# The turn from attention to the experts in a fused attention, soft mixture and gated layer: another order of its last round, and output weights that no longer stay on chip

## The chip, the cores and the metric

The kernel runs on one core of one Trainium2 chip. The metric is the device time of one execution in microseconds (us), as the median of several runs; lower is better. The core has TensorE for matrix products (PE below, with PEld for its weight loads), VectorE (DVE), ScalarE (ACT), GpSimd (POOL) and SyncE (SP), which issues all the transfers of this kernel. PE writes to PSUM alone; POOL does not reach PSUM.

## The reference

Three layers, one after the other. Attention with pooled queries (4 batches, 8 heads, 1152 keys, 576 pooled queries, 64 wide), a soft mixture of 8 experts of 4 slots each on 2304 tokens of 512, and a gated layer of width 1536 with a root-mean-square norm ahead of it:

```python
q_pool = q.reshape(B, H, S // 2, 2, D).mean(axis=3)
scores = scale * np.matmul(q_pool, k.transpose(0, 1, 3, 2))
scores = scores - np.max(scores, axis=-1, keepdims=True)
attn = np.exp(scores); attn = attn / (np.sum(attn, axis=-1, keepdims=True) + 1e-09)
x = heads_joined(np.matmul(attn, v))                  # 2304 x 512

logits = x @ phi                                      # 2304 x 32 slots
d = softmax over the tokens; slot_input = d.T @ x
slot_out[e] = np.maximum(slot_input[e] @ w1[e], 0.0) @ w2[e]
x = (softmax over the slots of logits) @ slot_out

xn = x / np.sqrt(np.mean(x * x, -1, keepdims=True) + 1e-06) * rms_g
g = xn @ w_gate
out = (g * (1.0 / (1.0 + np.exp(-g))) * (xn @ w_val)) @ w_out
```

All is float32. Products that need the full width are split by the kernel into a high and a low part, each rounded for PE's fast float32 form (fp32r), and are put together from two or three passes.

## The kernel before

**Attention** runs in 16 rounds, one for each pair of heads. In a round the scores (`sc`, L401) are taken tile by tile, ACT takes their exponentials (`e`, L403), PE multiplies these with the values (`av`, L424), and POOL, in the last round DVE too, adds them up for the sums (`acc`, L418). The work of the round before (its division, its logits) and the loads are hung into a round at places from a table of due times (`AT`). When the last round is over there is a stretch that nothing overlaps, here called the **turn**: it sums up the last round (`sums`), takes the last logits (`xl`, `by`, `z`, `lgt`), makes the last part of the softmax over the tokens (`dtx`, `dn`), multiplies it with the attention's output `xt` (`xo` is that output turned, L919 and L492 divide it) to the slot inputs (`pp`, `psb`, `pto`), and adds the earlier parts (`pt`, `mxw`).

**The experts** follow, one after another: a product with `w1` (`hin`, L984), a turn of the hidden row (`hto`, into a zeroed tile `hz`) and a product with `w2` (`so`, L1009). Between them PE turns the tokens' softmax for the next layer (`c4o`).

**The gated layer** comes last. The squares of its inputs (`x`, L1037, by DVE or ACT), their root (`rs`, POOL), the scaled weights of the tokens (`pt`, `c`, DVE and ACT), the gate and value weights for the slots (`part`, `sgo`, L1150 and L1157), the gate (`gv`, `th`, `hu`, its parts `hA`, `hW` and `hC`, L1202) and the products with the output weights (`yo`, L1219). An order written out by hand, `SEQ`, sets the first of its six groups of tokens: `p` is a pair of gate weights (`part`), `x` a square, `r` the root and scaled weights, `c` the turn of these, `o` the other half of a pair (`sgo`), `g` a gate, `y` the output product, `t` a call that issues loads, `s` a split of one output weight block into its parts `woh` and `wol`.

**The loads** all go through SP in one order. A block is 128 x 512 float32 (256 KB). The 128 expert blocks come in a stream, `w1` and `w2` of the experts in turn. Gate, value and output weights arrive as 64-bit numbers during attention and are narrowed there. What does not stay on chip is written to device memory (`away`) and read back behind the expert blocks. Before the change the output weights 0 to 3 stay on chip (`HELD_O`), so 32 of 36 narrowed blocks go out and come back. Room on chip is counted in buffers of four kinds: A, B, C and W. `KEEP` says how many B buffers are left free at a call of `load`. In the turn `load(40)` stands twice: behind `take_x`, with the tighter room of the last round, and behind `slot_copy`, which frees the two W buffers that held `xt`. In the expert stage four output blocks are split ahead (`EARLY`): their high parts on ACT (L1082), the low parts on POOL (L1083).

Of the kernel before, what the change touches and what calls it, by code (L numbers as in the profile page):

```python
# [113 lines left out]
SQ_DVE = (0, 2)  # L114
SP_ACT = (0, 1, 5, 4, 3, 2)
SEQ = "p0 t x0 x1 x2 x3 p1 t r o0 o1 p2 t c g0 o2 g1 p3 t g2 g3 y0 t y1 g4 s p4 t y2 g5 s o3 y3 s t s g6 s p5 y4 g7 o4 t o5 y5 g8 y6 g9 s g10 s y7 s y8 g11 s y9 y10 y11".split()
# [10 lines left out]
EARLY = 4  # L127
LEAD = 1
KEEP = [10, 6, 12, 12]
KEEP_A = [2, 0]  # L130
HELD = 0
HELD_O = 4
AHEAD_O = -1
# [10 lines left out]
def attention_softmoe_gated_kernel(ctx: ExitStack, tc: tile.TileContext, kT, qT, vv, ip, cst, w1, w2, wg, wv, wo, rg, out):  # L144
# [96 lines left out]
    def accum(name):  # L241
        return ps.tile([128, 512], F32, tag="av", bufs=2, name=name)

# [474 lines left out]
    def side(p):  # L718
# [69 lines left out]
        if p == NP - 1:  # L788
            at("load_15", lambda i: (keep_b.__setitem__(0, KEEP[0]), load(1, KEEP_A[1])))
        return sorted(todo, key=lambda x: x[:2])  # L790

    with tc.manual_schedule():
# [92 lines left out]
        l = NP - 1  # L885
        sums(l)
        take_x(l)
        load(40)
        recips(l)
        x_logits(l)  # L890
        o = xl.pop(l)
        xs = B([128, HQ], F32, "xs")
        ac.copy(xs, o)
# [3 lines left out]
        o = bank([128, HQ], "by")  # L897
        for t in range(3):
            for h in range(2):
                for i in range(2):  # L900
                    g = 64 * h + 32 * i
                    pe.matmul(o[g:g + 32, TB * t:TB * t + TB], lhsT=r[:, h, t, i:i + 1].to_broadcast([TB, 32]), rhs=ident[0:TB, 0:TB], start=True, stop=True)
        z = B([128, HQ], F32, "z")
        dv.tensor_tensor(out=z, in0=o, in1=xs, op=ALU.mult)
        rel("B", 2)
# [8 lines left out]
        x_turn_all(l)  # L914
        d_add(z, False)
        for i in range(3):
            for s in range(2):
                c = slice(64 * s, 64 * s + 64)
                ac.activation(xts[0][:, i, l % 4, c], xo[l, i][0][:, i, c], AF.Copy, scale=r[:, 0, i, s:s + 1])  # L919
# [3 lines left out]
        x_divide(l, range(3, 6))  # L923
        rel("B")
# [7 lines left out]
        d_copy(3)  # L932

# [28 lines left out]
        load(40)  # L962
        o = bank([128, 4, 32], "pto")
# [113 lines left out]
        def split_w():  # L1077
# [4 lines left out]
            ac.copy(woh[i], x)  # L1082
# [3 lines left out]
        def pull(n=0):  # L1086
            for _ in range(n):
                split_w()
            load(64)
# [5 lines left out]
        for e in range(NE):  # L1095
# [4 lines left out]
            if e + 1 < NE:  # L1100
                hs = expert_in(e + 1, lambda: z.append(expert_mid(e, last)))
                pull(EARLY // 2 if e > NE - 4 else 0)
# [140 lines left out]
        for step in SEQ:  # L1243
# [13 lines left out]
            elif step[0] == "t":  # L1257
                load(64)
            elif step[0] == "s":
# [56 lines left out]
```

## Time and profile before

| what | value |
|---|---|
| median of the runs before (3 runs) | 712.32 us (712.07 to 714.51) |
| profiled execution, its own time | 713.79 us |
| span of that execution, first to last instruction | 711.8 us |
| PE busy | 691.3 us (97%) |
| DVE, ACT, POOL busy | 456.6, 392.7, 434.5 us |
| mean granted clock of PE | 0.992 of 2.4 GHz |
| attention ends, the turn begins | about 451 us |
| first expert product starts | 466.15 us |
| last expert product ends | about 509.4 us |
| all gated work of one group after another, PE without idle time | from 529 us on |

A row of the timeline gives the start, the length, the engine, the line, the operation, and in brackets how long the engine stood idle before it and what ended that. Records of PE overlap, so the distance between two starts says more than a length. PEclk in a table of stretches is the granted clock as a share of 2.4 GHz: 1.00 is 2.4 GHz and 0.50 is 1.2 GHz. The DMA share is the mean busy share of the 16 DMA engines and can come out just above 1.

### The profile page before, as it was taken

The numbers are of one execution on the slowest core, as the hardware profiler recorded it, in microseconds if no ns is written. First come the engines' busy times: TensorE is split into PE (matmuls) and PEld (weight loads), VectorE is DVE, ScalarE is ACT, GpSimd is POOL, SyncE is SP. The second block draws the span as 40 slices with busy tenths as digits, with TensorE's granted clock in tenths as the row PEclk, the third lists the DMA queues.
The fourth block names the chain that finished last, engine by engine and source line by source line (L and its number), as shares of the span: only waits on it lengthen the run. The fifth ranks groups of instructions, "written<-read, shape, count | busy, mean of one in ns | idle before, by whom it ended". The sixth has DMA issues, their size and how long they took to land.

```text
span 711.8 us, 15218 instructions
## 1 busy us (share of the span) xinstructions
PE 691.3 (97%) x5948; PEld 481.8 (68%) x5948; DVE 456.6 (64%) x661; ACT 392.7 (55%) x831; POOL 434.5 (61%) x351
## 2 busy tenths in 40 slices
PE   4999999999999999999999999899999999999998
PEld 2566666666676666666666676454367888888887
DVE  5667888887877897787887766321255755534420
ACT  2465666766566766657756534423266855454420
POOL 5578888877787877787887675001237854534420
PEclk9999999999999999999999999889999999999999
DMA  5041642843844844835624416399970100000000
GB/s 181 21 180 59 218 143 93 292 143 107 307 143 137 270 136 138 283 118 186 204 92 158 154 48 224 120 352 389 387 264 1 44 30 17 29 30 31 23 34 34
DMA packets 53000, 103.57 MB, mean 145 GB/s; under 512 B 5832, under 2 KB 19648, under 8 KB 52928
## 3 DMA queue, kind: packets, MB, share of 16 engines
q1 hardware_dynamic: 52928, 102.59, 41.8%
q8 instruction: 47, 0.77, 0.5%
q14 instruction: 25, 0.20, 0.1%
HBM read 89.39 MB, written 13.11 MB: 144 GB/s over the span
## 4 chain that ended last, share of the span: by engine, by line
PE 92%; issue 2%; DVE 2%; DMA 1%; ACT 1%; POOL 1%; SPq 0%; POOLq 0%; ACTq 0%; DVEq 0%
PE sc L401 23%; PE av L424 21%; PE yo L1219 21%; PE mxp L344 5%; PE gv L1171 4%; PE hin L984 2%; PE xo L483 2%; PE so L1009 2%; PE sums L449 1%; PE xl L500 1%; PE mxp L354 1%; PE pp L562 1%; PE mxp L350 1%; DMA qraw<-in_qT_dram 1%; PE sumt L459 1%
## 5 line engine op out<-in xcount | busy, mean ns | idle before, releaser
L418 POOL TENSOR_TENSOR acc<-acc,e 128x576 f32<-128x576 f32 x153 | 215.3, 1427 | 32.9 <-ACT e L403 28.7
L403 ACT ACTIVATE e<-sc 128x576 f32<-128x576 f32 x288 | 163.8, 657 | 64.6 <-PE sc L401 63.8
L345 DVE TENSOR_REDUCE mx<-mxp 128x2 f32<-128x1024 f32 x120 | 143.8, 1223 | 61.5 <-PE mxp L344 61.0
L424 PE MATMUL av<-e,vt 128*64 128x288 f32 x1152 | 167.8, 417 | 0.0
L418 POOL TENSOR_TENSOR acc<-e 128x576 f32<-128x576 f32 x63 | 94.0, 1502 | 73.6 <-ACT e L403 73.5
L424 PEld LDWEIGHTS av<-e,vt 128*64 128x64 f32 x1152 | 72.6, 136 | 63.7 <-issue 28.9
L1219 PE MATMUL yo<-woh,hA 128*128 128x512 f32 (+1 forms) x312 | 98.9, 384 | 0.0
L401 PE MATMUL sc<-qh,kh 64*128 64x288 f32 x576 | 93.5, 321 | 0.4 <-ACT mrow L370 0.4
L401 PE MATMUL sc<-mr,pick 64*128 64x288 f32 x576 | 85.7, 294 | 0.0
L401 PE MATMUL sc<-qh,kl 64*128 64x288 f32 x576 | 85.7, 293 | 0.0
L401 PE MATMUL sc<-ql,kh 64*128 64x288 f32 x576 | 85.6, 293 | 0.0
L1176 DVE SCALAR_TENSOR_TENSOR th<-th,gv 128x384 f32<-128x384 f32 x72 | 39.9, 554 | 62.4 <-ACT th L1173 61.9
L1202 POOL TENSOR_TENSOR hA<-hu,hA 128x384 fp32r<-128x384 f32 x48 | 48.8, 1018 | 42.9 <-ACT hA L1201 39.2
L401 PEld LDWEIGHTS sc<-qh,kh 64*128 64x128 f32 x576 | 54.5, 185 | 19.3 <-issue 6.6
L1219 PEld LDWEIGHTS yo<-woh,hA 128*128 128x128 f32 x312 | 57.6, 188 | 10.2 <-issue 0.7
L1173 ACT ACTIVATE th<-gv 128x384 f32<-128x384 f32 x72 | 35.2, 489 | 42.4 <-PE gv L1171 39.7
L1219 PE MATMUL yo<-wol,hA 128*128 128x512 f32 (+1 forms) x151 | 57.8, 383 | 0.0
L401 PEld LDWEIGHTS sc<-qh,kl 64*128 64x128 f32 x576 | 55.0, 187 | 0.0
L401 PEld LDWEIGHTS sc<-mr,pick 64*128 64x128 f32 x576 | 54.8, 186 | 0.0
L401 PEld LDWEIGHTS sc<-ql,kh 64*128 64x128 f32 x576 | 54.7, 186 | 0.0
L344 PE MATMUL mxp<-kh,qh 64*128 64x512 f32 x240 | 47.8, 436 | 0.2 <-ACT kh L283 0.2
L1178 DVE SCALAR_TENSOR_TENSOR hu<-th,gv 128x384 f32<-128x384 f32 x72 | 39.9, 554 | 8.1 <-PE gv L1171 0.5
(198 smaller groups left out, 1044.5 us busy)
## 6 DMA issues: line engine op xcount, KB each, us to landing
w<-in_w_dram SPq DMA_DIRECT2D x88, 256.0 KB
w<-in_w_dram SPq DMA_DIRECT2D x20, 512.0 KB
vt<-in_vv_dram SPq DMA_DIRECT2D x16, 576.0 KB
qraw<-in_qT_dram SPq DMA_DIRECT2D x15, 576.0 KB
kraw<-in_kT_dram SPq DMA_DIRECT2D x15, 576.0 KB
away<-w SPq DMA_DIRECT2D x32, 256.0 KB
w<-away SPq DMA_DIRECT2D x32, 256.0 KB
raw<-in_wg_dram SPq DMA_DIRECT2D x12, 512.0 KB
```

The costliest lines, as they stand in the source:

```text
L344: pe.matmul(o[:, s, :], lhsT=q[r, 128 * t:128 * t + 128], rhs=k[r, 512 * c:512 * c + 512], start=True, stop=True)
L345: dv.reduce_max(out=heads[:, :, t, c], in_=o, axis=AX.X)
L401: pe.matmul(o[:, s, 0:HQ], lhsT=w[r, wk], rhs=q[r, c], start=(i == 0), stop=(i == 3))
L403: ac.activation(ets[p, kt, h], o[:, :, 0:HQ], AF.Exp, scale=0.0625)
L418: eng.tensor_tensor(out=acc[p, h, j], in0=first[p, h, j] if n == 1 else acc[p, h, j], in1=e, op=ALU.add)
L424: pe.matmul(avt[p, h][64 * s:64 * s + 64, 0:HQ], lhsT=vt[p][:, kt, 64 * s:64 * s + 64], rhs=ets[p, kt, h][:, s], start=(kt == 0), stop=(kt ...
L1171: pe.matmul(o[i], lhsT=sg[n][:, 256 * i + 128 * c:256 * i + 128 * c + 128], rhs=cT[g], start=True, stop=True)
L1173: ac.activation(t, o[0], AF.Tanh, scale=0.5)
L1176: dv.scalar_tensor_tensor(out=t, in0=t, scalar=1.0, in1=o[0], op0=ALU.add, op1=ALU.mult)
L1178: dv.scalar_tensor_tensor(out=u, in0=t, scalar=0.5, in1=o[1], op0=ALU.mult, op1=ALU.mult)
L1202: gp.tensor_tensor(out=b, in0=u, in1=f(a), op=ALU.subtract)
L1219: pe.matmul(o, lhsT=x, rhs=w[:, c], start=(ft == 0 and i == 0), stop=(ft == NF - 1 and i == 2))
```

## The change

Five things change together.

1. **The turn's order.** ACT copies the last outputs (`take_x`) ahead of the sums, PE turns them (`xo`) while ACT copies the sums, and the half that DVE divides (`x_divide`) stands ahead of `z`. `xl` and `by` use the two accumulator banks, which `av` no longer needs.
2. **Unread products in three waits.** `hold` issues PE products of 128 x 512 whose result nothing reads: seven behind the logits, two ahead of `pp`, two ahead of `pto`.
3. **No output weights held.** All 36 narrowed blocks go out and come back; the output weights come back between the pairs of gate weights. The expert blocks get the room: the `KEEP` numbers fall from 10 and 6 to 8 and 5, and the first `load(40)` of the turn already uses the 5.
4. **Splits.** The four splits of the expert stage go. Three new steps `w` in `SEQ` split output blocks 0 to 2, with both parts on POOL. The last `s`, until now without work, splits the last block.
5. **Squares.** Of the first group's four, only the first stays on DVE (before, the first and the third); the first pair's `sp` copy goes from ACT to DVE.

```diff
-SQ_DVE = (0, 2)
-SP_ACT = (0, 1, 5, 4, 3, 2)
-SEQ = "p0 t x0 x1 x2 x3 p1 t r o0 o1 p2 t c g0 o2 g1 p3 t g2 g3 y0 ...
+SQ_DVE = (0,)
+SP_ACT = (1, 5, 4, 3, 2)
+SEQ = "w p0 t x0 x1 x2 x3 p1 t r w w o0 o1 p2 t c g0 o2 g1 p3 t g2 g3 y0 ...
-EARLY = 4
-KEEP = [10, 6, 12, 12]
+KEEP = [8, 5, 12, 12]
-HELD_O = 4
-AHEAD_O = -1
+HELD_O = 0
+AHEAD_O = 1
+    def hold(o, n):
+        for _ in range(n):
+            pe.matmul(o, lhsT=pick[0], rhs=mr[1][:, 0:512], start=True, stop=True)
...
-            at("load_15", lambda i: (keep_b.__setitem__(0, KEEP[0]), load(1, KEEP_A[1])))
+            at("load_15", lambda i: (spill(), keep_b.__setitem__(0, KEEP[0]), load(1, KEEP_A[1])))
...
+        take_x(l)
         sums(l)
-        take_x(l)
+        x_turn(l, range(3))
+        x_turn(l, range(3, 6))
+        keep_b[0] = KEEP[1]
         load(40)
         recips(l)
-        x_logits(l)
-        o = xl.pop(l)
+        o = accum("xl")
...
+        x_divide(l, range(3, 6))
         z = B([128, HQ], F32, "z")
...
         d_add(lg[3], True)
-        x_turn_all(l)
         d_add(z, False)
+        busy = accum("hold")
+        hold(busy, 7)
...
         d_copy(3)
+        hold(busy, 2)
...
         load(40)
+        hold(busy, 2)
         o = bank([128, 4, 32], "pto")
...
-        def split_w():
+        def split_w(eng=None):
             i = min(n for n, i in w32 if i == 2)
             x, give = w32.pop((i, 2))
             woh[i], wol[i] = unit_r("woh"), unit_r("wol")
-            ac.copy(woh[i], x)
+            if eng is None:
+                ac.copy(woh[i], x)
+            else:
+                eng.tensor_copy(woh[i], x)
             gp.tensor_tensor(out=wol[i], in0=x, in1=f(woh[i]), op=ALU.subtract)
...
-                pull(EARLY // 2 if e > NE - 4 else 0)
+                pull()
...
+            elif step[0] == "w":
+                split_w(gp)
```

What stood on PE in the turn, from the sums' turn to the last product before the experts (names as in the section on the kernel; `sb` and `br` spread the softmax's scale):

```order
L459 MATMUL sumt<-cs,srow 96x128 x3
L500 MATMUL xl<-xu,ipt 64x288 x2
L902 MATMUL by<-cs,rr 32x96 x12
L911 MATMUL lgt<-lg,cs 32x288 x2
L483 MATMUL xo<-cs,xu 96x128 x6
L911 MATMUL lgt<-z,cs 32x288 x2
L545 MATMUL dn<-cs,dtx 96x32 x6
L562 MATMUL pp<-xt,dn 32x512 x4
L949 MATMUL sb<-st,cs 128x1
L562 MATMUL pp<-xt,dn 32x256 x4
L954 MATMUL br<-ad,ones 128x96
L965 MATMUL pto<-cs,psb 128x32 x4
```

What stands on PE now, from the turn of the outputs on:

```order
L479 MATMUL xo<-cs,xu 96x128 x6
L463 MATMUL sumt<-cs,srow 96x128 x3
L899 MATMUL xl<-xu,ipt 64x288 x2
L910 MATMUL by<-cs,rr 32x96 x12
L920 MATMUL lgt<-lg,cs 32x288 x2
L920 MATMUL lgt<-z,cs 32x288 x2
L246 MATMUL hold<-mr_82,pick_83 128x512 x7
L549 MATMUL dn<-cs,dtx 96x32 x6
L246 MATMUL hold<-mr_82,pick_83 128x512 x2
L566 MATMUL pp<-xt,dn 32x512 x4
L958 MATMUL sb<-st,cs 128x1
L566 MATMUL pp<-xt,dn 32x256 x4
```

`xo` has left the place between the two `lgt` pairs and stands ahead of `sumt`; the `hold` products are new, and the last two of them stand behind `br`, ahead of `pto`.

What SP issued in the turn before (`w1_...` and `w2_...` are buffers of the expert stream; 128x1024 and 128x2x512 are two blocks, 128x512 is one); the first four rows are the first `load(40)`, the rest the start of the second:

```order
L684 DMA w1_6530<-in_w1_dram 128x1024
L684 DMA w1_6532<-in_w1_dram 128x1024
L689 DMA w2_6534<-in_w2_dram 128x512
L689 DMA w2_6535<-in_w2_dram 128x512
L684 DMA w2_6631<-in_w2_dram 128x2x512
L684 DMA w2_6633<-in_w2_dram 128x2x512
L689 DMA w2_6631<-in_w2_dram 128x512
L689 DMA w2_6633<-in_w2_dram 128x512
```

What SP issues there now; the first eight rows are the first `load(40)`:

```order
L688 DMA w2_6558<-in_w2_dram 128x2x512
L688 DMA w2_6560<-in_w2_dram 128x2x512
L693 DMA w2_6562<-in_w2_dram 128x512
L693 DMA w2_6563<-in_w2_dram 128x512
L693 DMA w1_6566<-in_w1_dram 128x512
L693 DMA w1_6567<-in_w1_dram 128x512
L693 DMA w1_6570<-in_w1_dram 128x512
L693 DMA w1_6571<-in_w1_dram 128x512
L688 DMA w1_6670<-in_w1_dram 128x1024
L688 DMA w1_6672<-in_w1_dram 128x1024
```

The first `load(40)` now takes ten blocks where it took six, and six more have come ahead of it in the last rounds. From the second `load(40)` on, 62 of the 128 expert blocks were still to come before, and 52 are now.

What stood on POOL from the experts to the first gate parts before (`hz` is zeroed for an expert, `rs` is the root of the first group):

```order
L998 MEMSET hz 128x256 x6
L1083 TENSOR_TENSOR wol<-w_5371,woh 128x512
L1083 TENSOR_TENSOR wol<-w_5513,woh 128x512
L998 MEMSET hz 128x256
L1083 TENSOR_TENSOR wol<-w_5791,woh 128x512
L1083 TENSOR_TENSOR wol<-w_5923,woh 128x512
L998 MEMSET hz 128x256
L1054 TENSOR_TENSOR rs<-rs,half 96x4
L1202 TENSOR_TENSOR hC<-hu,hC 128x384
```

What stands on POOL now:

```order
L1008 MEMSET hz 128x256 x8
L1095 CAST woh<-w_6979 128x512
L1096 TENSOR_TENSOR wol<-w_6979,woh 128x512
L1064 TENSOR_TENSOR rs<-rs,half 96x4
L1095 CAST woh<-w_7075 128x512
L1096 TENSOR_TENSOR wol<-w_7075,woh 128x512
L1095 CAST woh<-w_7077 128x512
L1096 TENSOR_TENSOR wol<-w_7077,woh 128x512
L1213 TENSOR_TENSOR hC<-hu,hC 128x384
```

The last two `hz` no longer stand behind splits; one whole split stands ahead of `rs`, and two stand between `rs` and the first gate part.

## Rows read from the trace of the kernel before

**Rows 1.** Stretches: us, then busy time of PE, PEld, DVE, ACT, POOL; PEclk, DMA share, GB/s

```profile
458.00:460.00 2.00, 0.97 (x10) 0.72 (x14) 0.93 (x6) 1.34 (x6) 0.00 (x0) 0.68 0.01 4
460.00:462.00 2.00, 2.00 (x10) 0.34 (x2) 0.25 (x2) 0.00 (x0) 0.00 (x0) 0.50 0.04 8
466.00:502.00 36.00, 35.85 (x408) 16.10 (x410) 5.31 (x19) 11.42 (x32) 4.67 (x9) 0.96 1.05 388
529.00:700.00 171.00, 170.99 (x828) 142.02 (x821) 81.65 (x154) 90.14 (x212) 84.98 (x82) 1.00 0.07 25
```

**Rows 2.** Timeline of PE in the turn: start, length, line, idle before and what ended it

```profile
455.17 0.86 PE L483 MATMUL xo<-cs,xu 128*96 128x128 f32 x6
455.95 0.68 PE L911 MATMUL lgt<-z,cs 64*32 64x288 f32 x4
458.42 0.32 PE L545 MATMUL dn<-cs,dtx 32*96 32x32 f32 x3 [1.78 <-ACT dtx L928]
...
459.80 1.93 PE L562 MATMUL pp<-xt,dn 96*32 96x512 f32 x8 [0.46 <-ACT dn L552]
...
462.17 1.08 PE L562 MATMUL pp<-xt,dn 96*32 96x256 f32 x8
...
466.15 4.16 PE L984 MATMUL hin<-w,mxw 128*32 128x256 f32 x48 [0.38 <-DVE mxw L967]
470.24 0.44 PE L995 MATMUL hto<-cs,hs 128*128 128x128 f32 x2
```

**Rows 3.** Timeline of DVE in the turn

```profile
454.77 0.46 DVE L904 TENSOR_TENSOR z<-by,xs 128x288 f32<-128x288 f32 x1 [1.26 <-PE by L902]
...
463.83 0.48 DVE L573 TENSOR_SCALAR psb<-pp,wt 128x256 f32<-128x256 f32 x1 [1.39 <-ACT psb L572]
...
465.81 0.29 DVE L967 TENSOR_TENSOR mxw<-mxw,pto 128x128 f32<-128x128 f32 x1 [0.41 <-PE pto L965]
```

**Rows 4.** Timeline of PE: a 128x512 pair of the gated layer

```profile
524.23 0.62 PE L1219 MATMUL yo<-woh,hC 128*128 128x512 f32 x2
```

**Rows 5.** Timeline of PE: one middle expert, then the last two

```profile
477.64 1.92 PE L1009 MATMUL so<-w,hz 128*32 128x512 f32 x16
479.38 1.05 PE L984 MATMUL hin<-w,mxw 128*32 128x256 f32 x16
...
501.61 1.05 PE L1009 MATMUL so<-w,hz 128*32 128x512 f32 x4
...
504.51 3.58 PE L1009 MATMUL so<-w,hz 128*32 128x512 f32 x12 [0.48 <-DVE hz L999]
508.40 1.05 PE L1009 MATMUL so<-w,hz 128*32 128x512 f32 x4 [0.31 <-DMA w<-in_w_dram]
```

**Rows 6.** Timeline of SP's queue: the second load call of the turn

```profile
461.77 1.96 SPq L684 DMA_DIRECT2D w<-in_w_dram  x2
```

**Rows 7.** Timeline of PE, POOL and DVE where the gated layer starts

```profile
516.93 1.08 PE L1150 MATMUL part<-w,pt 128*32 128x128 f32 x32
518.30 0.65 PE L1030 MATMUL c4o<-identr,c 96*128 96x96 f32 x4 [0.28 <-DVE c L1024]
...
516.00 1.02 POOL L1054 TENSOR_TENSOR rs<-rs,half 96x4 f32<-96x4 f32 x1 [11.77 <-DVE rs L1053]
522.63 1.01 POOL L1202 TENSOR_TENSOR hC<-hu,hC 128x384 fp32r<-128x384 f32 x1 [5.61 <-ACT hC L1201]
...
517.82 0.42 DVE L1024 TENSOR_TENSOR c<-pt,c 96x256 fp32r<-96x256 f32 x1 [0.47 <-ACT c L1023]
```

**Rows 8.** DVE adds of two on-chip tiles: two beside POOL; all seven (min/median/max ns)

```profile
439.59 2.62 DVE L418 TENSOR_TENSOR acc<-acc,e 128x576 f32<-128x576 f32 x2 [1.74 <-POOL acc L418]
...
L418 DVE TENSOR_TENSOR acc<-acc,e x7: 746/751/1954, 432.9 to 449.6; 128x576 f32<-128x576 f32 x7
```

**Rows 9.** POOL's operations with one input or none: min/median/max ns

```profile
L998 POOL MEMSET hz<- x8: 306/312/313, 447.5 to 503.9; 128x256 f32 x8
L589 POOL COPY pair<-cs x2: 536/646/755, 94.0 to 94.6; 64x32 f32<-64x32 f32 x2
```

More of the change, by code (lines that the diff above doesn't have):

```diff
@@ L113 @@
 HALVED = (0,)
-SQ_DVE = (0, 2)
-SP_ACT = (0, 1, 5, 4, 3, 2)
-SEQ = "p0 t x0 x1 x2 x3 p1 t r o0 o1 p2 t c g0 o2 g1 p3 t g2 g3 y0 t y1 g4 s p4 t y2 g5 s o3 y3 s t s g6 s p5 y4 g7 o4 t o5 y5 g8 y6 g9 s g10 s y7 s y8 g11 s y9 y10 y11".split()
+SQ_DVE = (0,)
+SP_ACT = (1, 5, 4, 3, 2)
+SEQ = "w p0 t x0 x1 x2 x3 p1 t r w w o0 o1 p2 t c g0 o2 g1 p3 t g2 g3 y0 t y1 g4 s p4 t y2 g5 s o3 y3 s t s g6 s p5 y4 g7 o4 t o5 y5 g8 y6 g9 s g10 s y7 s y8 g11 s y9 y10 y11".split()
 SQUARE = {1: [12, 2, 24, 30], 2: [70, 80, 82, 104], 3: [7, 21, 33, 45], 4: [5, 17, 13, 41], 5: [5, 17, 29, 41]}
@@ L885, in attention_softmoe_gated_kernel @@
         l = NP - 1
+        take_x(l)
         sums(l)
-        take_x(l)
+        x_turn(l, range(3))
+        x_turn(l, range(3, 6))
+        keep_b[0] = KEEP[1]
         load(40)
         recips(l)
-        x_logits(l)
-        o = xl.pop(l)
+        o = accum("xl")
+        for h in range(2):
+            pe.matmul(o[64 * h:64 * h + 64, 0:HQ], lhsT=ipt[:, l % 4, :], rhs=xu[l][:, HQ * h:HQ * h + HQ], start=True, stop=True)
         xs = B([128, HQ], F32, "xs")
-        ac.copy(xs, o)
+        ac.copy(xs, o[:, 0:HQ])
         gm = S([32, 1], "gm")
@@ L896, in attention_softmoe_gated_kernel @@
         r = rr[l]
-        o = bank([128, HQ], "by")
+        o = accum("by")
         for t in range(3):
@@ L902, in attention_softmoe_gated_kernel @@
                     pe.matmul(o[g:g + 32, TB * t:TB * t + TB], lhsT=r[:, h, t, i:i + 1].to_broadcast([TB, 32]), rhs=ident[0:TB, 0:TB], start=True, stop=True)
+        x_divide(l, range(3, 6))
         z = B([128, HQ], F32, "z")
-        dv.tensor_tensor(out=z, in0=o, in1=xs, op=ALU.mult)
-        rel("B", 2)
+        dv.tensor_tensor(out=z, in0=o[:, 0:HQ], in1=xs, op=ALU.mult)
+        rel("B", 3)
         both = two_banks("lgt")
@@ L922, in attention_softmoe_gated_kernel @@
         dv.tensor_scalar(out=nm, in0=mall[:, 3:4], scalar1=gm, scalar2=-1.0, op0=ALU.max, op1=ALU.mult)
-        x_divide(l, range(3, 6))
-        rel("B")
         dtx[3] = B([32, 2, HQ], F32, "dtx")
@@ L1081, in split_w, with pull @@
             woh[i], wol[i] = unit_r("woh"), unit_r("wol")
-            ac.copy(woh[i], x)
+            if eng is None:
+                ac.copy(woh[i], x)
+            else:
+                eng.tensor_copy(woh[i], x)
             gp.tensor_tensor(out=wol[i], in0=x, in1=f(woh[i]), op=ALU.subtract)
             give()
-        def pull(n=0):
-            for _ in range(n):
-                split_w()
+        def pull():
             load(64)
```

## The prediction

> **What bounds the kernel now.** I read the table of stretches first, then the timelines of the turn, of the experts' end and of the gated layer's start. From 529 us on PE has no idle time (170.99 of 171.00 us, [rows 1]), so a shift of the gated layer's start reaches the end whole, and attention before the turn is not reordered. What can move lies between 451 and 529 us, in three places. In the turn PE waits 1.78 us for `dtx`, and the granted clock then falls: 0.68 in 458 to 460, 0.50 in 460 to 462 [rows 1, 2]. Its mean of 0.96 over 466 to 502 says that about 36 x 0.04 / 0.5 = 2.9 us of the experts also run at 1.2 GHz. Meanwhile the DMA engines stand almost still (shares of 0.01 and 0.04), though from 466 on they are full at 388 GB/s [rows 1]. Second, the last two experts wait for weights and for `hz` [rows 5]: their products end at 508.40 + 1.05 = 509.45. Third, the gated layer starts on a chain: root on POOL, `c` on DVE, `c4o` on PE [rows 7].
>
> **The turn's order.** `xo` stands between `z`'s end (454.77 + 0.46 = 455.23) and the product that reads it (455.95) [rows 2, 3]. Moved into the wait for the sums' copy it costs nothing there (its own wait, the copy of `xu`, comes first on ACT now), and `lgt` starts some 0.1 us after `z`. `x_divide` ahead of `z` is done while `xl` and `by` run. Gain 0.55 us, out of 0.3 to 0.72.
>
> **The unread products.** The nearest row is a pair of 128x512 in 0.62 us [rows 4], its first record 0.39, so one every 0.23: seven take 1.6 us in a wait of 1.78, two take 0.46 in the 0.46 ahead of `pp` [rows 2]. At 2.4 GHz they delay nothing. What they should save is the clock. Both halves of `pp` take 459.80 to 463.25 = 3.45 us, nearly all at half clock; from 459.25 at full clock I take 1.75, so they end at 461.0. ACT's half of `psb` comes first, and DVE starts 0.58 us after `pp` (463.83 against 463.25). From there to `hin` it is 463.83 to 466.15 = 2.32 us, of which 0.41 was the wait for `pto` at half clock [rows 2, 3]; at full clock, behind two unread products, `pto` (1.9 us at half) ends before DVE is there. So `hin` starts at 461.0 + 0.58 + 1.91 = 463.5. Its 48 records take 4.1 us to the `hto` [rows 2]; three times the 16 of a middle expert, at 1.05 [rows 5], are 3.1. `hto` comes at 466.6, not 470.24: **3.6 us**. If the clock falls in spite of them, their own time doubles and nothing is saved.
>
> **The loads.** SP's order leaves 52 expert blocks behind the second load call where it left 62. The four new blocks that go out do so inside attention's last rounds, where PE's products cover them, and I cost them at nothing; if one held up what stands behind it on SP, the price would be its own 0.68 us (0.262 MB at 388 GB/s [rows 1]). Ten blocks fewer are 10 x 0.68 = 6.8 us; that call waits for `pp` and so starts 2.1 us sooner than 461.77 [rows 6]. The last `w2` therefore lands 8.9 us sooner: the last product that waits for one starts at 499.5, not 508.40.
>
> **The experts' end.** Without waits PE would need 24 more records from 501.61 on: 1.5 x 1.92 = 2.9 us, ending at 504.5 and not 509.45 [rows 5]: 4.95 us. Less the 3.6 it ends at 500.9, its last half expert starting near 499.8: the blocks land just in time. The `hz` wait goes with the splits, which held POOL ahead of it. I take **4.8 us**, and 3.6 to 5.0 as bounds. Together the experts end 8.4 us sooner.
>
> **The gated layer's start.** Here some of it is given back. Three squares on ACT, none behind the first on DVE, let `rs` start about 0.2 us sooner; the second `sp` copy then comes 0.25 later, hidden by the next wait. One split stands ahead of `rs` on POOL, but its block lands right behind the first pair, near 503, and `rs` is due at 516.0 - 8.6 = 507.4. Two more stand directly behind `rs`, with `hC` queued behind them. While they run, DVE has `pt` and `c` to do, each from two tiles on chip. Beside POOL such an operation waits: the add takes 0.75 alone and 1.95 when POOL's next one started as it was released [rows 8]. So `pt` waits for the first copy (its time x) and ends near x + 0.35 after `rs`; the subtraction takes its turn then, 1.35 by `hC` (1.01 for 384 [rows 7]), and `c`, 0.42 long, waits for that: it ends x + 2.1 us after `rs` instead of 518.24 - 517.02 = 1.2. The trace has no such copy: below it lies a zeroing of 256 in 0.31, so 0.62 for 512 [rows 9]; above it the two-input 1.35. I take x = 1.0, nearer the upper since it also reads. So `c4o` is late by 1.9 - 0.2 = 1.7 us against the shift: 518.30 - 8.4 + 1.7 = 511.6. The transfers reach `part` of the third pair, 15 blocks behind the last `w2`, at 499.5 + 10.1 = 509.6, against 516.93 - 8.4 = 508.5; it ends at 510.7, inside that same wait. The later pairs have more room. `hC` is due at 522.63 - 6.7 = 515.9, and POOL is free near 514.
>
> This is what the Trainium skill (SBUF — State Buffer, section "Who interferes with whom") states: an instruction of VectorE with two SBUF inputs is shut out while one of GpSimd that reads SBUF runs. The trace agrees [rows 8]. By the skill's GPSIMD Engine Reference (section 3.1), a one-input loop over 512 elements took 769 ns; no run here shows it, and the sum by it would be 0.2 us better.
>
> **The sum.** 3.6 + 4.8 - 1.7 = 6.7 us. The profiled execution of 713.79 us becomes 707.1; it lies 1.47 above the median of 712.32, from which I predict **705.6 us**. The extra `s`, one cast and one subtraction in a stretch where ACT and POOL are half busy (90 and 85 of 171 us, [rows 1]), costs nothing unless the last product catches it up.
>
> **The rivals.** (a) *The clock falls anyway*, in spite of the unread products. Then the turn is about as long as before (0.55 won, two late pairs at half clock lost, some 0.55 later in all by the last pair), the experts' end still wins 5 with blocks in time, and 1.7 goes back: 5.0 - 0.5 - 1.7 = 2.8, **709.5**. For it: in 460 to 462 PE was busy 2.00 of 2.00 and got no clock back. Against it: the fall followed the one long wait. (b) *The loads bind*: the call starts no sooner, or the queue is not full at once. Then the experts end 6.8 sooner by the ten blocks alone, less 1.7: **707.2**. For it: blocks and products meet within 0.3 us in my sum. (c) *POOL does not shut DVE out*, since `pt` gets in first: then the transfers set the third pair at -7.3 and little is given back: **704.7**. Against it: [rows 8]. (d) *The copy on POOL is dear.* Its only one-input copy took 0.54 to 0.76 us for 32 elements [rows 9]; if that were a price by element, 512 would take 10 us. Each us of x is paid in `c`; above about 3.1 again in `rs` behind the first split (due at 507.4, block there near 503), above about 3.4 a third time in `hC`. At x = 4.7 the whole gain is gone; at 10 it is some 16 us **slower**, near 729. Against it: POOL's subtractions write the same format at 1.01 for 384, so most of those 0.65 us is a fixed part. (e) That the change does not do what it says is part of (a).
>
> **Chances.** Forecast 0.55, (c) 0.14, (b) 0.14, (a) 0.12, (d) 0.05. The range reaches from 703.6 (`c` unhindered and the clock kept) to 709.6 (just (a)); outside lie (d), half of (a) and a small part of (c). A measurement here tells about 0.5% from no change, 3.6 us: faster is below 708.8. Forecast, (b), (c) and a third of (a) are faster, 0.87; the rest of (a) and (d) up to x near 5.9 are the same, 0.09; slower keeps 0.04.
>
> **What would show it.** Clock: a granted clock of 1.00 through 458 to 466 and `hin` near 463.5; 0.50 there is (a). Loads: SP's second call near 459.7 and no DMA wait at the last `so`; if those stay, (b). POOL: `pt` or `c` longer than the 0.42 of before or starting late, and `c4o` waiting for `c` by more than 0.28; if not, (c). CAST rows on POOL give x, and above 4 us (d). I am wrong if attention's last rounds grow, if the experts' middle pitch changes, or if PE shows idle time after the first group.

## The result and the profile after

The changed kernel takes 707.06 us (706.80 to 707.72); the kernel before, run beside it, has a median of 713.41 over all its runs. The ratio is 0.991, with a 95% interval of 0.989 to 0.994: faster by 0.9%. The profiled execution took 706.80 us (span 705.0, before 711.8), so the span is 6.8 us shorter, where the steps of the prediction added up to 6.7.

The stretches of the kernel after, with the columns of [rows 1]:

```profile
458.00:460.00 2.00, 2.00 (x20) 0.61 (x18) 0.79 (x5) 0.07 (x1) 0.00 (x0) 1.00 0.03 8
460.00:462.00 2.00, 2.00 (x16) 1.64 (x12) 1.19 (x3) 0.47 (x1) 0.00 (x0) 1.00 0.68 190
466.00:502.00 36.00, 35.23 (x383) 14.80 (x383) 4.97 (x18) 9.15 (x27) 2.06 (x7) 1.00 1.02 378
```

The granted clock, which stood at 0.68, 0.50 and 0.96 in [rows 1], is now 1.00 (2.4 GHz) in all three. The DMA engines still stand almost still from 458 to 460, but they are at work again two us sooner.

PE in the turn, answering to [rows 2]:

```profile
454.43 0.68 PE L920 MATMUL lgt<-z,cs 64*32 64x288 f32 x4
455.04 1.88 PE L246 MATMUL hold<-mr,pick 128*128 128x512 f32 x7
456.87 0.80 PE L549 MATMUL dn<-cs,dtx 32*96 32x32 f32 x6
...
458.26 1.06 PE L566 MATMUL pp<-xt,dn 96*32 96x512 f32 x8
...
462.80 2.80 PE L994 MATMUL hin<-w,mxw 128*32 128x256 f32 x48 [0.74 <-DVE mxw L977]
465.52 0.44 PE L1005 MATMUL hto<-cs,hs 128*128 128x128 f32 x2
```

The 1.78 us ahead of `dn` are filled by the seven `hold` products; the first half of `pp` takes 1.06 us where it took 1.93, and `hin` 2.80 where it took 4.16.

The end of the experts and the start of the gated layer on PE, POOL and DVE, answering to [rows 5] and [rows 7], and the call of SP that answers to [rows 6]:

```profile
496.89 2.94 PE L1019 MATMUL so<-w,hz 128*32 128x512 f32 x20
500.14 1.05 PE L1019 MATMUL so<-w,hz 128*32 128x512 f32 x4 [0.30 <-DMA w<-in_w_dram]
...
510.28 0.43 PE L1161 MATMUL part<-w,pt 128*32 128x128 f32 x8 [0.26 <-DMA w<-away]
510.76 0.65 PE L1040 MATMUL c4o<-identr,c 96*128 96x96 f32 x4
...
515.95 0.40 PE L1230 MATMUL yo<-woh,hC 128*128 128x512 f32 x1
...
459.37 1.75 SPq L688 DMA_DIRECT2D w<-in_w_dram  x2
...
507.49 1.02 POOL L1064 TENSOR_TENSOR rs<-rs,half 96x4 f32<-96x4 f32 x1 [1.92 <-DVE rs L1063]
508.47 0.61 POOL L1095 CAST woh<-w 128x512 fp32r<-128x512 f32 x1
509.16 1.27 POOL L1096 TENSOR_TENSOR wol<-w,woh 128x512 fp32r<-128x512 f32 x1
510.37 0.81 POOL L1095 CAST woh<-w 128x512 fp32r<-128x512 f32 x1
...
508.55 0.68 DVE L1066 TENSOR_TENSOR pt<-cn,rs 96x128 f32<-96x128 f32 x1 [1.13 <-POOL rs L1064]
509.70 1.01 DVE L1034 TENSOR_TENSOR c<-pt,c 96x256 fp32r<-96x256 f32 x1 [0.47 <-DMA w<-away]
```

The last product still waits for a block; it ends at 501.19 where it ended at 509.45. `c` takes 1.01 us and not 0.42 [rows 7], and ends 0.28 us behind the subtraction on POOL that ran beside it (509.16 + 1.27 = 510.43). Yet `c` alone does not hold PE: its last `part` product of the third pair waits for a transfer and ends at 510.71, when `c` ends too.

**Where the 6.8 us lie.** The starts of some steps cut the execution into seven pieces. `sums` is the first product of the turn, `hto` the first turn of a hidden row, "end" the end of the last `so`, `y0` the first output product, "the last gate product" the start of the last pair of `gv`.

| piece | before | after | difference | forecast |
|---|---|---|---|---|
| start to `sums` | 450.94 | 450.22 | -0.72 | 0 |
| `sums` to `hto` | 19.30 | 15.30 | -4.00 | -3.6 |
| `hto` to end | 39.21 | 35.67 | -3.54 | -4.8 |
| end to `c4o` | 8.85 | 9.57 | +0.72 | +1.7 |
| `c4o` to `y0` | 5.24 | 5.19 | -0.05 | 0 |
| `y0` to the last gate product | 159.34 | 159.87 | +0.53 | 0 |
| from there to the end of the span | 28.92 | 29.18 | +0.26 | 0 |

The total is right, but four terms differ from the forecast, in both directions. The first row isn't the work of the change: up to the turn PE has the same instructions in the same order in all kernels here, and in the executions below `sums` starts anywhere from 449.71 to 451.26. In every profile this difference to the kernel before is there at 25 us already and changes by less than 0.1 us from there to `sums`, so the additional transfers in attention's last rounds cost PE nothing. The third to sixth rows are what most of the experiments are about. The last row lies behind PE: its last product ends 25.9 us behind the last gate product in both kernels, and the 0.26 us come in what closes the program. What sets them no run here shows.

### The profile page after: what moved, and what is told of

Its sections match the earlier page's. It is cut to its first block, busy times and chain, and to the rows that moved or that the text cites. A ratio compares the mean times of both kernels' runs of the same rounds, so it can differ in the third digit from the quotient of the medians.

```text
span 705.0 us, 15269 instructions
## 1 busy us (share of the span) xinstructions
PE 687.5 (98%) x5959; PEld 481.2 (68%) x5959; DVE 457.1 (65%) x659; ACT 391.4 (56%) x829; POOL 436.0 (62%) x354
## 4 chain that ended last, share of the span: by engine, by line
PE 89%; DMA 5%; DVE 3%; ACT 2%; issue 1%; SPq 0%; DVEq 0%; ACTq 0%
PE sc L405 23%; PE av L428 22%; PE yo L1230 20%; PE mxp L348 5%; PE gv L1182 3%; DMA w<-away 2%; DMA w<-in_w_dram 2%; PE xo L487 2%; PE sums L453 1%; PE hin L994 1%; PE mxp L358 1%; PE xl L504 1%; PE so L1019 1%; PE mxp L354 1%; PE pp L566 1%; DMA qraw<-in_qT_dram 1%
## 5 line engine op out<-in xcount | busy, mean ns | idle before, releaser
L1187 DVE SCALAR_TENSOR_TENSOR th<-th,gv 128x384 f32<-128x384 f32 x72 | 39.8, 553 | 63.0 <-ACT th L1184 62.5
```

The source lines that it names most:

```text
L1187: dv.scalar_tensor_tensor(out=t, in0=t, scalar=1.0, in1=o[0], op0=ALU.add, op1=ALU.mult)
```

## The experiments

Times are medians with their range; the ratio is to the kernel before, run beside the kernel (its median there: 713.41 for the changed kernel, 712.37 for e1 to e4, 713.28 for e5, e6, e8 and e9, 712.16 for e7 and e10 to e12). The four columns behind it are pieces of the table above, from each kernel's profiled execution; they leave out the start, which differs by up to 1.5 us between executions of the same attention. These medians of the kernel before differ by more than 1 us, so between kernels that ran beside different ones of them the ratios say more than the times.

| kernel | us | ratio, 95% interval | `sums` to `hto` | `hto` to end | end to `c4o` | `sums` to `y0` |
|---|---|---|---|---|---|---|
| before | | | 19.30 | 39.21 | 8.85 | 72.60 |
| after | 707.06 (706.80 to 707.72) | 0.9912 (0.9887 to 0.9938) | 15.30 | 35.67 | 9.57 | 65.73 |
| e1, no unread products | 708.71 (707.22 to 709.64) | 0.9946 (0.9924 to 0.9967) | 17.33 | 34.15 | 9.61 | 66.26 |
| e2, turn alone | 711.23 (710.52 to 713.40) | 0.9979 (0.9966 to 0.9992) | 15.34 | 42.90 | 8.84 | 72.32 |
| e3, loads alone | 709.69 (708.71 to 711.40) | 0.9955 (0.9942 to 0.9969) | 19.94 | 34.15 | 9.59 | 68.86 |
| e4, early casts on ACT | 707.09 (705.60 to 707.75) | 0.9917 (0.9893 to 0.9942) | 15.30 | 34.86 | 9.44 | 66.30 |
| e5, last split earlier | 706.79 (706.19 to 708.38) | 0.9906 (0.9889 to 0.9922) | 15.30 | 35.73 | 9.58 | 67.04 |
| e6, two more blocks ahead | 706.52 (705.95 to 707.75) | 0.9907 (0.9891 to 0.9923) | 15.35 | 34.32 | 9.58 | 64.43 |
| e7, seven unread products only | 708.01 (707.66 to 708.24) | 0.9944 (0.9929 to 0.9958) | 17.70 | 34.15 | 9.61 | 66.64 |
| e8, output blocks later | 706.16 (705.97 to 707.23) | 0.9903 (0.9888 to 0.9917) | 15.30 | 34.34 | 8.62 | 63.51 |
| e9, e5 + e6 + e8 | 705.42 (704.90 to 706.92) | 0.9891 (0.9877 to 0.9906) | 15.35 | 34.15 | 8.67 | 63.45 |
| e10, the two pairs only | 710.42 (706.05 to 711.91) | 0.9965 (0.9945 to 0.9984) | 19.28 | 34.39 | 9.60 | 68.45 |
| e11, squares back | 707.23 (707.01 to 708.01) | 0.9935 (0.9920 to 0.9950) | 15.31 | 34.59 | 9.83 | 64.88 |
| e12, e9 without unread products | 709.48 (709.07 to 709.89) | 0.9964 (0.9951 to 0.9977) | 18.62 | 34.15 | 9.60 | 67.55 |

### Do the unread products keep the clock? (e1, e7, e10)

e1 takes out all eleven:

```diff
-        busy = accum("hold")
-        hold(busy, 7)
...
-        hold(busy, 2)
...
-        hold(busy, 2)
```

> The changed kernel without its eleven unread products; all else stays. Theory (they hold the granted clock, and the clock is worth something): the clock falls to about 0.5 between 458 and 462 as in the kernel before, pp ends some 2.1 us later, hin starts some 2.5 to 3 us later, the second load call some 2 us later, and the experts' end and the whole run come some 2.4 us later, near 709.5. Rival 1 (the new order alone keeps the clock, or the clock never mattered since the loads set the experts' end): hin within 0.5 us of the changed kernel and the time near 707. Rival 2 (the unread products themselves delay something): the run gets faster than 707.

The stretches of e1:

```profile
458.00:460.00 2.00, 1.94 (x19) 0.68 (x19) 0.76 (x4) 0.01 (x1) 0.00 (x0) 0.97 0.03 8
460.00:462.00 2.00, 2.00 (x10) 1.83 (x9) 1.39 (x3) 0.48 (x1) 0.00 (x0) 0.50 0.84 240
462.00:464.00 2.00, 1.62 (x15) 0.97 (x18) 0.81 (x3) 0.00 (x0) 0.00 (x0) 0.50 1.01 355
```

The clock does fall, but in this execution only at the end of `pp`, so `hin` starts at 462.89, 0.09 behind the changed kernel. Its 48 records run at 1.2 GHz, `hto` comes 2.0 us later (17.33 against 15.30), and 1.5 of these come back in the experts, which now wait for no block (34.15 against 35.67). The profiled execution is the shortest of e1 (707.22); its others lie up to 709.64, and where the clock fell in those, no profile shows. But the mean granted clock was recorded for each execution, and the times follow it: 0.995 in the profiled one, 0.993 at 708.38 and 708.71, 0.990 at 709.56 and 709.64, against 0.998 to 1.000 in the four executions of the changed kernel. Rival 1 is wrong about the clock, and nearly right about that one execution. The intervals of the two ratios overlap; that the unread products pay is shown by e12 against e9, below.

e7 keeps the seven alone, e10 the two pairs alone:

> The changed kernel with the seven unread products behind the logits alone; the two ahead of pp and the two ahead of pto are taken out. Theory (the one long wait, 1.8 us for dtx, is what the clock falls after; the two short ones, 0.46 and 0.4 us, do not matter): the granted clock is 1.00 from 456 to 466, hin starts within 0.1 us of the changed kernel and the time is 707.1 within 0.4. Rival (all three waits have to be filled): the clock falls at some place between 458 and 466 and the time is near that of the kernel without unread products, 708.7.

> The changed kernel with the two pairs of unread products alone; the seven behind the logits are taken out, so PE waits 1.8 us for dtx again. Theory (the long wait decides): the granted clock falls to 0.50 somewhere behind 458 as in the kernel without unread products, and the executions spread from 707.2 to 709.6, median near 708.7. Rival (short products in the later waits are enough): clock 1.00 and 707.1.

The stretches of e7:

```profile
458.00:460.00 2.00, 1.54 (x17) 0.58 (x17) 1.05 (x6) 0.34 (x2) 0.00 (x0) 1.00 0.01 5
460.00:462.00 2.00, 1.79 (x15) 1.21 (x15) 0.97 (x3) 0.48 (x1) 0.00 (x0) 0.82 0.45 143
462.00:464.00 2.00, 1.62 (x14) 1.26 (x17) 1.39 (x4) 0.00 (x0) 0.00 (x0) 0.50 1.04 347
```

and of e10:

```profile
458.00:460.00 2.00, 2.00 (x19) 0.56 (x11) 0.38 (x2) 0.00 (x0) 0.00 (x0) 0.82 0.17 25
460.00:462.00 2.00, 2.00 (x7) 1.64 (x7) 1.45 (x3) 0.47 (x1) 0.00 (x0) 0.50 0.86 258
```

My theory for e7 fell. With the long wait filled the clock still fell, near 461.3, behind short waits of 0.46 us ahead of `pp` and 0.21 ahead of `pto`, and `hto` came 2.4 us later; the time is 0.9 above the changed kernel, and its range begins (707.66) where that kernel's ends (707.72), though the intervals of the ratios overlap. The mean clock is 0.995 in all four of its executions. For e10 the theory held in the profile: the fall comes near 459.3, in `pp`, and the second pair then runs at half clock itself. The times were missed: a median of 710.42 where 708.7 was expected, and the widest range of all, 706.05 to 711.91. Here too they follow the mean clock, from 1.000 at 706.05 and 0.998 at 706.84 to 0.990 at 711.91. So with the long wait open the clock falls in most executions, but not in all, and with the long wait closed and the two short ones open it fell in all four. Both are needed. The pairs alone gain nothing over no unread products at all (710.42 against 708.71, intervals of the ratios overlapping).

### What does each half give alone? (e2, e3)

e2 is the kernel before with the turn's order and the unread products alone, e3 the kernel before with the other three parts alone (`KEEP`, `HELD_O`, `AHEAD_O`, `SEQ`, splits and squares).

> The kernel before with only the turn changed (new order, x_divide ahead of z, unread products); output weights 0 to 3 held, loads, splits and squares as before, so 62 expert blocks are behind the second load call. Theory (the loads set the experts' end): hin starts some 4 us sooner than in the kernel before, but the last product waits for its block, which lands only as much sooner as the second load call goes out, 2.1 to 2.4 us; the run gains about 2.2 us, near 710. Rival (the turn's gain reaches the end whole): 4 us, near 708.4. Rival 2 (nothing without the loads): 712.3 or more.

> The kernel before with only the loads, the splits and the squares changed; the turn in its old order and without unread products, so 52 expert blocks are behind the second load call. Theory (PE then sets the experts' end): the granted clock falls in the turn as before, hin starts at its old place, the last product of the experts ends some 4.9 us sooner than in the kernel before and waits for no block; some 0.7 us is given back at the gated layer's start and 0.5 us at the last split, so 3.7 us are gained, near 708.6. Rival (the loads are worth nothing while the turn is slow): within 1 us of 712.3. Rival 2 (the loads alone are the whole gain): near 706.5.

The experts' end in e2 on PE:

```profile
498.55 1.15 PE L1019 MATMUL so<-w,hz 128*32 128x512 f32 x4 [2.01 <-DMA w<-in_w_dram]
...
503.97 1.05 PE L1019 MATMUL so<-w,hz 128*32 128x512 f32 x4 [0.29 <-DMA w<-in_w_dram]
...
507.94 1.05 PE L1019 MATMUL so<-w,hz 128*32 128x512 f32 x4 [0.31 <-DMA w<-in_w_dram]
```

and in e3:

```profile
469.73 0.45 PE L995 MATMUL hto<-cs,hs 128*128 128x128 f32 x2
...
501.10 2.78 PE L1009 MATMUL so<-w,hz 128*32 128x512 f32 x24
...
513.47 0.65 PE L1030 MATMUL c4o<-identr,c 96*128 96x96 f32 x4 [0.89 <-DVE c L1024]
```

In e2 the turn is 4.0 us shorter, and the experts are 3.7 us longer: almost the whole gain turns into waits for blocks (and into a granted clock of 0.67 in 498 to 502, within these waits). Over its runs e2 gains 0.2% (0.1 to 0.3), some 1.5 us where 2.2 had been expected; the profiled execution is its longest, 2.2 us above its median, so in the others less may turn into waits. In e3 PE runs through to the end with no wait: 34.15 us from `hto`, the forecast's floor (504.5 - 470.24 = 34.3), and 0.4% (0.3 to 0.6) or 3.2 us are gained (3.7 expected). Together the halves give 0.9%, more than 0.2 and 0.4, but the three intervals leave room for a plain sum. In the profiles the difference is plain: from `sums` to `y0` the turn alone gives 0.3 us, the loads alone 3.7 and both 6.9, since each takes away the limit that hides part of the other. The part of this that comes from e2's long execution is not known.

### Do the blocks still bind? (e6, e12)

e6 lets the first load call of the turn fill the room down to three buffers:

```diff
         x_turn(l, range(3, 6))
-        keep_b[0] = KEEP[1]
+        keep_b[0] = 3
         load(40)
```

> The changed kernel with two more expert blocks in the first load call of the turn (50 and not 52 behind the second call). Theory (the blocks meet the products at the end of the experts, and whether they bind depends on the rate that the DMA engines give in that execution): no DMA wait at the last products whatever the rate, the experts end 2.7 us after the last w2 product series begins (about 499.7 us), so 0 us sooner than the changed kernel where the rate is near 386 GB/s and 1.4 us sooner where it is near 376; the time falls by 0 to 1 us, 706.6 taken. Rival 1 (the loads never bound): no change in any row. Rival 2 (two more blocks in flight in the turn delay something there): hin later, the time above 707.1.

PE at the end of the experts in e6, and in e5, which loads its expert blocks as the changed kernel does:

```profile
497.39 2.95 PE L1019 MATMUL so<-w,hz 128*32 128x512 f32 x24
```

```profile
500.67 1.05 PE L1019 MATMUL so<-w,hz 128*32 128x512 f32 x4 [0.28 <-DMA w<-in_w_dram]
```

From `hto` to the end e6 takes 34.32 us, 1.35 less than the changed kernel, and its last 24 products follow each other without a break. In the profiled execution of the changed kernel the last blocks did bind, by 1.5 us against the 34.15 that PE takes where it waits for none (e1, e3). How much of that the two blocks take away one profile of e6 cannot tell: in the other profiles with the changed kernel's order of expert blocks the piece is 34.34 (e8), 34.59 (e11), 34.86 (e4) and 35.73 us (e5), so how much the blocks bind differs between executions. The median moves by 0.5 us, within the ranges.

e12 is e9 (below) without the unread products, and asks what the clock is worth once the blocks are out of the way:

> The kernel with all three later edits (last split earlier, two more blocks ahead, output blocks 1 and 2 behind the third pair) without any of the eleven unread products. Theory (what the clock is worth depends on the loads: where the blocks bind, part of a later start is hidden in their waits; here they do not bind): the clock falls, hto comes some 2 us later and the end of the experts as much, so the time is 707.4 to 708.4, over 2 us above 705.4. Rival (the unread products are not needed any more once the loads are out of the way): 705.4 within 0.4.

PE in e12:

```profile
458.41 1.94 PE L566 MATMUL pp<-xt,dn 96*32 96x512 f32 x8 [0.46 <-ACT dn L556]
...
464.81 4.39 PE L990 MATMUL hin<-w,mxw 128*32 128x256 f32 x48 [0.38 <-DVE mxw L973]
469.12 0.44 PE L1001 MATMUL hto<-cs,hs 128*128 128x128 f32 x2
...
512.87 0.65 PE L1036 MATMUL c4o<-identr,c 96*128 96x96 f32 x4 [0.90 <-DVE c L1030]
```

It is 4.1 us slower than e9 (5.2 by the ratios), more than I expected, and the intervals are far apart. The mean clock is 0.993 at most in all five executions, and 0.998 to 1.000 in those of e9. In the profiles `hto` comes 3.3 us later, nothing of it comes back in the experts (34.15 in both), and 0.9 more is lost at `c4o`, since PE is now late, the output blocks are there when POOL comes to them, and its splits shut DVE out again. So a lost clock costs between 0.5 us (e1's profile, its shortest execution, `sums` to `y0`, where the blocks bind) and 4 us (e12, where they do not).

### POOL and DVE ahead of `c4o` (e4, e8)

e4 gives the casts of the three early splits to ACT, e8 reads the output blocks 1 and 2 back behind the third pair of gate weights:

```diff
-                split_w(gp)
+                split_w()
```

```diff
-        while n < min(NF, AHEAD_O + 2 * i):
+        while n < min(NF, max(AHEAD_O, 2 * i - 1)):
```

> The changed kernel with the casts of the three early splits on ScalarE and not on GpSimd (the subtractions stay on GpSimd). Theory (GpSimd shuts VectorE out of its two-input operations, but the third pair's transfers hide it): pt of the scaled weights takes about 0.29 us again and not 0.68, c ends some 1 us sooner after rs, and yet c4o starts within 0.1 us of the changed kernel, behind the last part of the third pair; the time stays at 707.1 within 0.3. Rival 1 (the shutting out was on the path): c4o some 1 us sooner, 706.1. Rival 2 (it is not GpSimd's reading that lengthens pt and c): they stay at 0.68 and 1.01.

> The changed kernel with the output blocks 1 and 2 read back behind the third pair of gate weights and not ahead of it. Theory (two limits lie on top of each other at the third pair: its transfers, and c, which waits for GpSimd's splits): the third pair lands 1.4 us sooner, the two splits start only when their blocks land, some 2 us after rs, so pt takes 0.29 and c 0.42 us again, c4o starts about 0.9 us sooner against the end of the experts (8.7 us behind it and not 9.6), and hC still finds GpSimd free; the time falls by 0.6 to 0.9 us, to about 706.3. Rival 1 (the splits now run into hC): y0 no sooner, 707.1. Rival 2 (only one of the two limits goes): half the gain or less.

DVE and PE in e4:

```profile
507.75 0.29 DVE L1066 TENSOR_TENSOR pt<-cn,rs 96x128 f32<-96x128 f32 x1 [1.13 <-POOL rs L1064]
508.50 0.42 DVE L1034 TENSOR_TENSOR c<-pt,c 96x256 fp32r<-96x256 f32 x1 [0.47 <-ACT c L1033]
...
509.47 0.43 PE L1161 MATMUL part<-w,pt 128*32 128x128 f32 x8 [0.25 <-DMA w<-away]
509.82 0.65 PE L1040 MATMUL c4o<-identr,c 96*128 96x96 f32 x4
511.39 1.01 PE L1182 MATMUL gv<-cT,sg 128*128 128x384 f32 x2 [0.92 <-ACT cT L1043]
```

and DVE, POOL and PE in e8:

```profile
508.26 0.29 DVE L1066 TENSOR_TENSOR pt<-cn,rs 96x128 f32<-96x128 f32 x1 [1.13 <-POOL rs L1064]
508.51 1.08 PE L1161 MATMUL part<-w,pt 128*32 128x128 f32 x32
...
509.02 0.42 DVE L1034 TENSOR_TENSOR c<-pt,c 96x256 fp32r<-96x256 f32 x1 [0.47 <-ACT c L1033]
509.43 0.61 POOL L1095 CAST woh<-w 128x512 fp32r<-128x512 f32 x1 [1.20 <-DMA w<-away]
...
509.52 0.65 PE L1040 MATMUL c4o<-identr,c 96*128 96x96 f32 x4
```

In both, `pt` is back at 0.29 us and `c` at 0.42, so it was POOL's splits that lengthened them. In e4 `c` ends at 508.92 and yet `c4o` starts at 509.82, behind the last transfer of the third pair, only 0.13 sooner against the end than in the changed kernel. Two limits lay on top of each other; e8 takes both away (its `part` of the third pair runs through, 32 products in 1.08 us) and gains 0.95 (8.62 against 9.57), the 0.9 that was expected. In its profile e4 loses behind `c4o`: ACT is late with `cT`, the granted clock falls to 0.60 in 511 to 513 and 0.55 in 513 to 515, and `c4o` to `y0` takes 6.70 us instead of 5.19. That the late `cT` costs the clock is not shown: e5's profile has the same fall (below) with nearly the waits of the changed kernel (0.62 us ahead of `gv` in both). Of e4's four executions two kept a mean clock of 1.000 and took 705.60 and 706.67, two had 0.998, the profiled one among them, and took 707.50 and 707.75. What e4 is worth where the clock stays is open.

### The last split (e5), the squares (e11), and all three edits (e9)

In the changed kernel PE waits at 550 us. Rows of its ACT and PE, and of ACT in the kernel before:

```profile
547.92 0.61 ACT L1093 CAST woh<-w 128x512 fp32r<-128x512 f32 x1
548.44 0.48 ACT L1184 ACTIVATE th<-gv 128x384 f32<-128x384 f32 x1
...
550.23 0.45 PE L1182 MATMUL gv<-cT,sg 128*128 128x384 f32 x1 [0.21 <-DVE hu L1189]
```

```profile
555.50 0.48 ACT L1173 ACTIVATE th<-gv 128x384 f32<-128x384 f32 x1
```

The extra cast stands where `th` stood before (in the kernel before it follows the same high part of a gate directly, at 555.50, and this place lies 7.58 us sooner now, at 547.92). `th` is 0.52 us late, the gates' banks come free as much later, and everything on PE behind it too. The same 0.5 us stand in the profiles of all the kernels with this split in this place (e1, e3, e4, e6, e7, e8, e10 and e11), and not in e2, which has none there. e5 puts that split between the high parts of the last two gates of the group:

```diff
-... s y7 s y8 g11 s y9 y10 y11
+... s y7 s y8 g11 y9 y10 y11
...
             if fts[-1] == NF - 1:
+                if g == 0:
+                    split_w()
                 gate_parts(g, NF - 1)
```

> The changed kernel with its last split one place earlier on ScalarE, in the idle time between the last two high parts of the first group's gates. Theory (the extra split's cast, 0.61 us, pushed the tanh behind it by 0.52 us and PE waited for the gate's banks): th behind it starts 0.5 us sooner, the gv of the second group at 549.6 us waits no more, and everything behind it comes 0.5 us sooner; the time falls from 707.1 to about 706.5. Rival (the wait at 549.6 us has another cause, GpSimd's two low parts in a row): the wait stays, or moves behind the split, and the time stays at 707.1.

From `y0` to the last gate product e5 takes 159.67 us (before 159.34, after 159.87): 0.2 of the 0.53 come back, which the medians don't resolve (e9 and e12, with the same edit, take 159.65 and 159.69). Up to 36 us behind `y0` it is level with the kernel before (35.46 against 35.41 for the same gate; 35.94 in the changed kernel), and 0.3 are lost some 8 us later. So the cause is the one named, but the extra work on ACT and POOL finds another place to wait. In its profiled execution, besides, the granted clock fell to 0.50 in 513 to 515, and `c4o` to `y0` took 6.43 us; that makes its `sums` to `y0` long and lies ahead of the place of the edit.

e11 puts the squares and the first `sp` copy back:

```diff
-SQ_DVE = (0,)
-SP_ACT = (1, 5, 4, 3, 2)
+SQ_DVE = (0, 2)
+SP_ACT = (0, 1, 5, 4, 3, 2)
```

> The changed kernel with the squares and the first sp copy back at their old engines (first and third square on VectorE, the first sp copy on ScalarE). Theory: rs starts about 0.2 us later, c with it, and c4o by no more than that, since it stands behind the third pair's transfers or within 0.2 us of them; the time is 707.1 to 707.3. Rival (the new places are worth more, since ScalarE or VectorE stood in the way of the first pair): over 0.5 us later at c4o.

From the end of the experts to `c4o` it takes 9.83 us and not 9.57: 0.26 later, as foreseen; the time tells nothing of that size.

> The three preceding edits together in the changed kernel: the last split one place earlier, two more expert blocks ahead, output blocks 1 and 2 behind the third pair. Theory (three separate places, so the gains add up): 0.5 + 0.8 + 0 to 1.4 us, about 705.1 (704.4 to 705.8). Rival (each gain is given back at the next limit): 706 or more.

e9 is the fastest, 705.42 us, 1.1% under the kernel before, and within what was expected. In its profile 2.3 us are gained on the changed kernel between `sums` and `y0` (63.45 against 65.73): 1.5 at the experts' end and 0.9 at `c4o`, less 0.1 elsewhere. Behind `y0` 0.2 more are won up to the last gate product, and 0.4 lost again behind the last product of PE; e6 and e12, which also load the two blocks sooner, lose the same 0.4 there. The cause is open. The medians differ by 1.6, and the intervals of the two ratios overlap, so what the times alone show is that it is not slower.

## Why the prediction was right, and where its steps were not

The time lies in the range and 1.5 us above the number. Of these, 1.1 lie in the start: the median of the kernel before was 712.32 for the prediction and is 713.41 with the run that came to it. On the profiled execution the span fell by 6.8 us where the sum was 6.7, which is in part luck, as the steps show:

- **The order of the turn.** `pp` starts 8.86 us behind `sums` before and 8.04 after: 0.8 and not 0.55, a little over my bound of 0.72. e1, with the new order and no unread product, has it at 7.91, and e3, with the old order, at 9.00. So the order is worth about 1 us, and the two unread products ahead of `pp` take 0.13 of it back, where I had said that they delay nothing.
- **The clock.** Kept, as forecast, and e1, e7 and e12 show that without the unread products, or with the seven alone, it falls in every execution, and e10 that with the pairs alone it falls in most. `hin` starts 2.63 us sooner against `sums`, where 2.65 was forecast; its 48 records gave 1.37 more and not 1.0, since they were faster than three times a middle expert (2.73 us to `hto`, not 3.1). What I had not seen is how little of this a slower clock would have cost in some executions: in e1's profile the blocks hide three quarters of it. The rival (a) asked the right question; its price lies between 0.5 and 4 (I had 3.9).
- **The loads.** The call went out at 459.37, where I had 459.7, but only because this execution was 0.72 ahead at `sums`. From `sums` the call took 9.15 us and not 8.76: it came 1.7 sooner and not 2.1. From the call to the last product it took 40.77 us, and the step "the last `w2` therefore lands 8.9 us sooner" made that 39.8. This is the term that was mis-sized: 3.54 and not 4.8. With blocks and products meeting within 0.3 us, as the prediction said, both errors went into waits. I had taken 388 GB/s from one execution; the changed kernel's profile shows 378 over the same stretch, and in 36 us that makes 0.9. It is not the whole cause: e5, with 384 GB/s there, needed 40.83 from its call. What else held the blocks up is open. Rival (b) happened in part, at a price of 1.5 us (35.67 against 34.15).
- **The gated layer's start.** The direction was right: POOL's splits do shut `pt` and `c` out (e4, e8), `c` ends 2.2 us behind `rs` and not 1.2, and the squares give 0.25 back (e11). The size was not, +0.72 and not +1.7, for two reasons: x, the copy of 512 elements on POOL, took 0.61 us, just under my lower bound of 0.62, where I took 1.0; and `c` was free 0.5 sooner than x + 2.1 says, above all since the subtraction behind the copy did not wait for `pt` (it started at 509.16, `pt` ran to 509.23). The transfers of the third pair, which I had ending 0.9 ahead of `c`, ended together with it, and it took e8 to remove both limits. Rivals (c) and (d) are refuted by `c` at 1.01 and by x. The Trainium skill (GPSIMD Engine Reference, section 3.1) gives 769 ns for a loop over 512 elements. The rows show 0.61 us, and 0.81 for a copy that stood beside `c`; the rows decide. The rule that the prediction cited from the Trainium skill (SBUF — State Buffer, "Who interferes with whom") agrees with every row of `pt` and `c` in e4, e8 and the changed kernel.
- **The extra split.** The step that costed it at nothing failed. It rested on the share of a long stretch in which ACT is half busy [rows 1]; but the group's last gates are a chain of ACT, DVE and PE without slack, and there one cast of 0.61 us cost 0.53. Idle time of PE after the first group, which the prediction named as a sign of being wrong, did show: 0.21 us at 550.
- **What no step had.** 0.72 us of the profiled difference were won ahead of the turn, in the first 25 us, by instructions that did not change. That is luck, and against the errors above it made the sum look better than its terms: without it the change gave 6.1 us of span, which is also nearer to the medians (6.35 against the runs beside it, 5.3 against those shown before).

## What to carry to other kernels

Before a gain is counted, ask which limit lies just behind it: here the turn alone gave 0.2%, the loads alone 0.4%, and both 0.9%, and in the profiles each hid part of the other. Where two waits end within 0.3 us of each other in a sum, take a rate or a start from several executions, since one execution's rate and start decide the sign of the slack. And cost a moved operation by the queue that it enters and what stands behind it there, not by the busy share of the stretch around it.

## What the runs showed of the hardware

- The granted clock fell to half after waits far shorter than the long one: in e7 no wait of PE between the logits and the fall was longer than 0.46 us. And with the wait of 1.8 to 2.0 us ahead of `dn` it fell at different places: worked out from the granted clock of the stretches, near 457.8 in e12 (0.96 in 456 to 458), and by that of 458 to 460 near 458.7 before (0.68), 459.3 in e10 (0.82), 459.6 in e3 (0.89) and 459.9 in e1 (0.97): ahead of `pp`, within it and at its end. In two of ten executions of e10 the mean clock was 0.998 or more. The times of e1 and e10, which spread by 2.4 and 5.9 us where the changed kernel's spread by 0.9, go with the mean clock of each execution. What sets the moment of the fall, these runs leave open.
- The rate of the DMA engines between 466 and 502 was 388 GB/s before, 378 after and 385 in e1; after and e1 issue the same stream of blocks. Over all profiles it lies between 372 (e12) and 388. The cause is open.
- Ahead of the turn, executions of the same PE instructions differ by up to 1.5 us at `sums`. For the two profiles of before and after the difference arises here, in the first products with the values:

```profile
19.82 1.23 PE L424 MATMUL av<-e,vt 128*64 128x288 f32 x4
20.98 0.99 PE L324 MATMUL mxp<-kh,qh 64*128 64x384 f32 x4
```

is the kernel before, and

```profile
19.83 0.92 PE L428 MATMUL av<-e,vt 128*64 128x288 f32 x4
20.68 0.62 PE L328 MATMUL mxp<-kh,qh 64*128 64x384 f32 x4
```

the kernel after: the same products, slower in the first by 0.3 and 0.4 us, while the granted clock reads 1.00 in both. A pair of score products (`sc`, 288 columns each) starts every 0.24 us at 18.9 us in both and every 0.13 at 24 us, and PE passes from the slow pace to the fast one near 19 us in e10, 20.3 after, 21.7 before and 22 in e8, in the order of their `sums`. So PE changes its pace at a different moment in each of these executions, and the recorded granted clock does not show it; why is open.
